# Projecting the last tokens of four segments, not two, in one job of the idle columns, with filling matmuls, an earlier layernorm and a deferred weight load

## The chip, the cores and the metric

One core of a Trainium2 chip. The metric is the device time of one execution in microseconds (us). A kernel's figure is the median of its runs. Every run in this document fell in the fast state, so all comparisons are of like with like.

## The reference, cut to what matters

Four layers run in a row, A B A B, on a residual stream of 2048 tokens by 640. Layer A is attention with a compressive memory and isn't touched by the change. Layer B carries its memory from one segment of 32 tokens to the next:

```python
for s in range(64):                                   # 2048 / 32
    h = concatenate([mem, x[:, 32*s:32*s+32]])        # 8 + 32 = 40 tokens
    q, k, v = h @ Wq, h @ Wk, h @ Wv                  # 640 -> 32 heads x 128
    p = softmax(where(mask, q @ k.T / sqrt(128), -1e9))
    o = (p @ v) @ Wo                                  # 40 x 640
    mem = o[:, :8]                                    # the next segment needs this
    outs.append(o[:, 8:])
# x = x + A(ln(x)); x = x + B(ln(x)); twice
```

## The kernel before

A step of layer B projects 32 columns for the queries and keys: the 8 memory rows and the first 24 tokens of the *next* segment. They are ready as soon as the memory is. The last 8 tokens of a segment (its tails) don't fit into the 32 columns and don't depend on the memory, so they are projected ahead in jobs of four units (two for Q, two for K) of 20 matmuls each. A job has room for 32 columns; before, it fills 16 of them with the tails of two segments:

```python
def make_tails_job(t):
    segs = [u for u in (t, t + 1) if u < nsteps]
    hx = wk.tile([128, NCH, 32], BF16, name="b_hx")
    for ii, u in enumerate(segs):
        nc.gpsimd.tensor_copy(hx[:, :, 8 * ii:8 * ii + 8], xcols(u, 24, 32))
    ...
```

The part of a step on which everything below turns, with the names that the profile uses:

```python
V2 = v_quarter(2); V3 = v_quarter(3)
...                                              # softmax: P is normalised by GpSimd and DVE
if len(bulk) > 0:
    bulk_unit_pe(bulk[0][0], bulk[0][1])         # first unit of tails: b_tps, 20 matmuls
ptp = ps_tile([128, 8, 128], BF16, "b_PTP")      # one tile in PSUM
for t in range(8):
    nc.tensor.transpose(ptp[:, t, :], P[...], C.identb[:])
nc.vector.tensor_copy(PTsb[:, 0:4, :], ptp[:, 0:4, :])
nc.scalar.copy(PTsb[:, 4:8, :], ptp[:, 4:8, :])
if len(bulk) > 1:
    bulk_unit_pe(bulk[1][0], bulk[1][1])         # second unit of tails
# OTP: 32 matmuls, probabilities x V; OTsb: evacuation on DVE and ACT
# OPS: 64 matmuls with Wo; msb (ACT), MT (transposes the new memory), hT, next step
```

Steps 0 and 63 of a layer have no units; steps 1 to 62 have two. Every fourth step also has a block OPSd, which does the output projection of 4 x 8 rows that no later step waits for. P are the probabilities, PTP their transposes, and PTsb the copy of PTP that OTP reads. All results of matmuls land in PSUM tiles here; copying one out to SBUF is called its evacuation. A matmul is called cold where the granted clock was 0.5, and warm where it was 1.00.

Of the kernel before, what the change touches and what calls it, by code (L numbers as in the profile page):

```python
# [18 lines left out]
F32 = mybir.dt.float32  # L19
BF16 = mybir.dt.bfloat16  # L20
# [9 lines left out]
NCH = 5  # L30
# [445 lines left out]
    pass  # L476


def load_B_weights(nc, tc, ctx, B_Wq, B_Wk, B_Wv, B_Wo):
    wp = ctx.enter_context(tc.tile_pool(name="b_w", bufs=1))  # L480
    W = BWeights()
    for nm, src in (("wq", B_Wq), ("wk", B_Wk), ("wv", B_Wv)):
        t = wp.tile([128, NCH, 4096], BF16, name=f"b_{nm}")
        nc.sync.dma_start(t[:], src.rearrange("(c p) h e -> p c (h e)", p=128))
        setattr(W, nm, t)
    W.wo = wp.tile([128, 32, D], BF16, name="b_wo")
    nc.sync.dma_start(W.wo[:], B_Wo.rearrange("h e d -> e h d"))
    return W


# [6 lines left out]
def layer_B(nc, tc, C, W, x_src, xb_src, x_dst, mem0, nsteps=64, out_bf16=False, dbg=None):  # L497
# [3 lines left out]
    with ExitStack() as ctx:  # L501
        st = ctx.enter_context(tc.tile_pool(name="b_state", bufs=1))
        hp = ctx.enter_context(tc.tile_pool(name="b_hT", bufs=4))
        qkp = ctx.enter_context(tc.tile_pool(name="b_qk", bufs=4))
        wk = ctx.enter_context(tc.tile_pool(name="b_wk", bufs=1))
        wk2 = ctx.enter_context(tc.tile_pool(name="b_wk2", bufs=2))
        sm = ctx.enter_context(tc.tile_pool(name="b_sm", bufs=2))
# [9 lines left out]
        nc.vector.tensor_tensor(out=fold[:, 0, :], in0=C.identb[:, 0:32], in1=C.identb[:, 64:96], op=ALU.add)  # L517
        nc.vector.tensor_tensor(out=fold[:, 1, :], in0=C.identb[:, 32:64], in1=C.identb[:, 96:128], op=ALU.add)
        OTdef = st.tile([128, 32, 32], BF16, name="b_OTdef")
        XO = st.tile([128, 320], F32, name="b_XO")  # L520
        nc.vector.memset(XO[:], 0.0)
        mask8 = st.tile([128, 8, 40], BF16, name="b_mask8")
# [21 lines left out]
        def ln_group_a(g):  # L544
            if g not in ln_dma:
                ln_group_dma(g)
            xt = ln_dma.pop(g)
            xn = wk.tile([128, D], BF16, name="b_xn", tag="PTsb")
            layernorm_tile(nc, sm, C, xt[:], xn[:], "b_ln")
            ln_state[g] = xn  # L550

        def ln_group_b(g):
            xn = ln_state.pop(g)
            tps = ps_tile([128, NCH, 128], BF16, "b_lntps")
            for c in range(NCH):
                nc.tensor.transpose(tps[:, c, :], xn[:, 128 * c:128 * c + 128], C.identb[:])
            xg = wk2.tile([128, NCH, 128], BF16, name="b_xnTg")
            nc.scalar.copy(xg[:], tps[:])
            xnT_g[g] = xg

        def xcols(s, a, b):
            g, i = divmod(s, 4)
            return xnT_g[g][:, :, 32 * i + a:32 * i + b]
# [54 lines left out]

        def bulk_unit_evac(job, u, eng):
            nm, b = (("Q", 0), ("Q", 1), ("K", 0), ("K", 1))[u]  # L620
            sb = wk.tile([128, 512], BF16, name="b_tsb", tag="tsb")
            evac(eng, sb[:], job["ps"][u][:], SCB if nm == "Q" else None)
            job["sb"][u] = sb

# [3 lines left out]
            transp4(job["sb"][u][:], tp, 0)  # L628
            job["tp"][u] = tp

        def bulk_unit_scatter(job, u, eng):
            nm, b = (("Q", 0), ("Q", 1), ("K", 0), ("K", 1))[u]
            for (t0, t1, seg, c0) in job["dests"]:
                dst_t = (QT if nm == "Q" else KT)[seg]
                src = job["tp"][u][:, 0:4, :].rearrange("p i (j t) -> p i j t", j=4)[:, :, :, t0:t1]
                dst = dst_t[:, 0:1280].rearrange("p (h c) -> p h c", c=40)[:, 16 * b:16 * b + 16, c0:c0 + (t1 - t0)] \
                    .rearrange("p (j i) c -> p i j c", j=4)
                evac(eng, dst, src)

        def new_job(cols, dests):  # L640
            return {"cols": cols, "dests": dests, "ps": {}, "sb": {}, "tp": {}}

        def run_job_now(job):
            for u in range(4):
                bulk_unit_pe(job, u)
                bulk_unit_evac(job, u, "act" if u % 2 == 0 else "dve")
                bulk_unit_tr(job, u)
                bulk_unit_scatter(job, u, "dve" if u % 2 == 0 else "act")

        ln_group_a(0); ln_group_b(0)  # L650
        alloc_seg(0)
        with nc.allow_non_contiguous_dma(reason="mem0 transpose load (tiny)"):
# [1 line left out]
                nc.sync.dma_start(hT[0][:, c, 32:40], mem0[:, 128 * c:128 * c + 128].rearrange("t p -> p t"))  # L654
        if nsteps > 1:
            alloc_seg(1)
        run_job_now(new_job(hT[0][:, :, 0:32], [(0, 32, 0, 0)]))

        def make_tails_job(t):
            segs = [u for u in (t, t + 1) if u < nsteps]  # L660
            hx = wk.tile([128, NCH, 32], BF16, name="b_hx")
            nc.gpsimd.memset(hx[:], 0.0)
            dl = []
            for ii, u in enumerate(segs):
                nc.gpsimd.tensor_copy(hx[:, :, 8 * ii:8 * ii + 8], xcols(u, 24, 32))
                dl.append((8 * ii, 8 * ii + 8, u, 24))
            return new_job(hx[:], dl)

        if nsteps > 1:
            if nsteps > 2:  # L670
                alloc_seg(2)
            run_job_now(make_tails_job(1))
        if nsteps > 4:
            ln_group_a(1); ln_group_b(1)
        jobs = {}
        pend_ln_b = []

        for s in range(nsteps):
            last = (s == nsteps - 1)
            if s + 2 < nsteps and (s + 2) not in hT:  # L680
                alloc_seg(s + 2)
            t_a = s + 2 if (s + 2) % 2 == 1 else None
            t_b = s + 1 if (s + 1) % 2 == 1 else None
            bulk = []
            if t_a is not None and t_a >= 3 and t_a < nsteps:
                if t_a + 1 < nsteps and (t_a + 1) not in hT:
                    alloc_seg(t_a + 1)
                jobs[t_a] = make_tails_job(t_a)
                bulk = [(jobs[t_a], 0), (jobs[t_a], 1)]
            if t_b is not None and t_b >= 3 and t_b in jobs:  # L690
                bulk = [(jobs.pop(t_b), 2), (jobs[t_b] if False else None, 3)]
                bulk[1] = (bulk[0][0], 3)
            g_need = (s + 6) // 4
            do_ln = None
            if g_need * 4 < nsteps and g_need not in xnT_g and g_need not in ln_state and g_need not in pend_ln_b:
                do_ln = g_need
# [14 lines left out]
            evac("dve", Ksb[:, 1, :], Kb[:])  # L711
            while pend_ln_b:
                ln_group_b(pend_ln_b.pop(0))
            Vsb = wk.tile([128, 4, 512], BF16, name="b_Vsb", tag="Vsb")

            def v_quarter(b4):
# [57 lines left out]
            evac("act", Vsb[:, 3, :], V3[:])  # L774
            if len(bulk) > 0:
                bulk_unit_pe(bulk[0][0], bulk[0][1])
            ptp = ps_tile([128, 8, 128], BF16, "b_PTP")
            for t in range(8):
                nc.tensor.transpose(ptp[:, t, :], P[:, 2 * t:2 * t + 2, :].rearrange("p g k -> p (g k)"), C.identb[:])
# [41 lines left out]
            nc.gpsimd.tensor_copy(OTdef[:, :, 8 * (s % 4):8 * (s % 4) + 8], OTsb[:].rearrange("p (h c) -> p h c", c=40)[:, :, 0:8])  # L821
            tsb = None
            if bulk:
                tsb = wk.tile([128, 2, 512], BF16, name="b_tsb", tag="Ksb")
                for i, (job, u) in enumerate(bulk):
                    nm = "Q" if u < 2 else "K"
                    evac("act" if i == 0 else "dve", tsb[:, i, :], job["ps"][u][:], SCB if nm == "Q" else None)
                    job["sb"][u] = tsb[:, i, :]
# [24 lines left out]
                pend_ln_b.append(do_ln)  # L853
            if bulk:
                for i, (job, u) in enumerate(bulk):
                    nm, b = (("Q", 0), ("Q", 1), ("K", 0), ("K", 1))[u]
                    for (t0, t1, seg, c0) in job["dests"]:
                        dst_t = (QT if nm == "Q" else KT)[seg]
                        src = btp[:, 4 * i:4 * i + 4, :].rearrange("p i (j t) -> p i j t", j=4)[:, :, :, t0:t1]
                        dst = dst_t[:, 0:1280].rearrange("p (h c) -> p h c", c=40)[:, 16 * b:16 * b + 16, c0:c0 + (t1 - t0)] \  # L860
                            .rearrange("p (j i) c -> p i j c", j=4)
                        evac("act" if i == 0 else "dve", dst, src)
            if out_bf16:
                xnb = wk.tile([128, 320], BF16, name="b_xnb", tag="xnb")
                nc.vector.tensor_tensor(out=xnb[0:64, :], in0=xps[0:64, :], in1=XO[0:64, :], op=ALU.add)
# [32 lines left out]
def full_kernel(tc, A_x, A_wq, A_wk, A_wv, A_wo, A_beta, B_x, B_mem0, B_Wq, B_Wk, B_Wv, B_Wo, B_seg_len, out, layers="ABAB"):  # L898
    nc = tc.nc
    with ExitStack() as ctx:  # L900
        C = build_consts(nc, tc, ctx)
        xin = A_x.rearrange("b s d -> (b s) d")
        xout = out.rearrange("b s d -> (b s) d")
        mem0 = B_mem0.rearrange("b t d -> (b t) d")
        X = tc.dram_tile([S_TOK, D], F32, name="xres")
        Xb = tc.dram_tile([S_TOK, D], BF16, name="xres_bf")
        nl = len(layers)
        assert layers[0] == "A"
        for li, L in enumerate(layers):
            lastl = (li == nl - 1)  # L910
            if L == "A":
                with ExitStack() as actx:
                    WA = load_A_weights(nc, tc, actx, C, A_wq, A_wk, A_wv, A_wo, A_beta)
                    layer_A(nc, tc, C, WA, xin if li == 0 else X, xout if lastl else X, li == 0, out_bf16=lastl,
                            xb_dst=None if lastl else Xb)
            else:
                with ExitStack() as bctx:
                    WB = load_B_weights(nc, tc, bctx, B_Wq, B_Wk, B_Wv, B_Wo)
                    layer_B(nc, tc, C, WB, X, Xb, xout if lastl else X, mem0, out_bf16=lastl)


# [56 lines left out]
```

## Time and profile before

| | before |
|---|---|
| time, median of 4 runs | 3668.54 us (3663.58 to 3669.13) |
| span of the profiled execution | 3666.6 us |
| TensorE busy | 3329.6 us, 91% |
| period of steps 1 to 60 of layer B, by step number modulo 4 (0, 1, 2, 3) | 19.26, 19.14, 19.14, 22.19 us |
| those 120 steps together | 2391.5 us |
| tails matmuls (b_tps with b_hx) | 5120 |

The periods are from the start of one step's first Q projection to the next's, medians over both layers. The 22.19 contains OPSd and the layernorm's transposes. All changes of the granted clock in this trace lie 3.41 us or a multiple of it apart: it is 1.00 from 3649.43 to 3652.84, for one, and 0.50 from there to 3656.25. So stretches of that length are used below to look at it. TensorE's 91% invites the conclusion that a matmul removed is time gained. The prediction's first part reads the lines that say otherwise: within a step TensorE is busy partly because work that nobody waits for has been put where it would wait.

### The profile page before, as it was taken

To read this page: it belongs to the slowest core of one execution; us is meant where nothing else is said; L and a number is where in the kernel's file an instruction comes from. 1 tells how busy PE (TensorE), PEld (TensorE's weight loads), DVE (VectorE), ACT (ScalarE), POOL (GpSimd) and SP (SyncE) were. 2 spreads that over 40 slices of the span, in tenths; PEclk is the share of its full clock that TensorE was granted. 3 is DMA by queue.
4 is the path that set the end of the run, shared out by engine and by line. 5 is a ranking of instruction groups with operands and counts; after the bars stand their busy time and mean duration, and the time that the engine had idled before them with its cause. 6 is when DMAs were issued, how large, how long until landed. Compare 5 with 4: busy or idle time off the path is not lost.

```text
span 3666.6 us, 126376 instructions
## 1 busy us (share of the span) xinstructions
PE 3329.6 (91%) x54996; PEld 2072.5 (57%) x54996; DVE 2032.9 (55%) x5299; ACT 1852.8 (51%) x4369; POOL 580.5 (16%) x1457
## 2 busy tenths in 40 slices
PE   6988959999999999999869889599999999999998
PEld 4756635555555555555546666355555555555555
DVE  8888834444444444444479888344444444444443
ACT  5978834444444444444359788344444444444443
POOL 4233210110111111010122332101101111110100
PEclk9999979999999999999989999799999999999999
DMA  2010061000000000000020111600000000000000
GB/s 63 12 38 30 29 248 31 12 12 13 13 13 12 14 13 12 14 12 10 20 66 12 46 38 29 249 29 10 10 11 11 11 11 11 11 10 12 10 8 8
DMA packets 85996, 112.24 MB, mean 31 GB/s; under 512 B 27328, under 2 KB 75456, under 8 KB 81600
## 3 DMA queue, kind: packets, MB, share of 16 engines
q1 hardware_dynamic: 85440, 104.18, 9.1%
q8 instruction: 429, 7.03, 0.8%
q14 instruction: 127, 1.04, 0.1%
HBM read 72.13 MB, written 23.59 MB: 26 GB/s over the span
## 4 chain that ended last, share of the span: by engine, by line
PE 74%; ACT 12%; DVE 7%; issue 3%; DMA 2%; POOL 2%; SPq 0%; DVEq 0%; ACTq 0%; POOLq 0%
PE b_VPS L103 16%; PE b_tps L103 9%; PE b_OPS L103 8%; ACT a_Pj L338 5%; PE b_Qa L103 4%; PE b_Qb L103 4%; PE b_Kb L103 4%; PE b_Ka L103 4%; PE a_S L333 3%; ACT b_KT L103 2%; PE b_ttp L103 2%; PE b_PTP L103 2%; PE b_TPK L103 2%; PE b_TPQ L103 2%; PE b_OPSd L103 2%
## 5 line engine op out<-in xcount | busy, mean ns | idle before, releaser
L103 PEld LDWEIGHTS <-b_hT 128*32 128x32 bf16 (+1 forms) x15520 | 608.4, 101 | 498.2 <-issue 99.8
L103 PE MATMUL b_VPS<-b_wv,b_hT 128*64 128x512 bf16 x5120 | 626.3, 382 | 0.0
L338 ACT ACTIVATE a_Pj<-a_S,a_negm 128x128 bf16<-128x128 f32 (+3 forms) x1024 | 504.1, 541 | 50.0 <-DVE a_negm L337 43.9
L337 DVE TENSOR_REDUCE a_negm<-a_S 128x1 f32<-128x128 f32 (+3 forms) x1024 | 467.5, 481 | 76.6 <-PE a_S L335 47.9
L103 ACT CAST b_Vsb<-b_VPS 128x512 bf16<-128x512 f32 x512 | 289.3, 594 | 179.6 <-PE b_VPS L103 179.6
L103 POOL TENSOR_TENSOR b_P<-b_P,b_rs 128x320 bf16<-128x320 bf16 x128 | 92.4, 722 | 1799.6 <-DVE b_rs L103 1785.0
L333 PE MATMUL a_S<-a_kT,a_qTm 128*128 128x128 bf16 (+3 forms) x1024 | 292.2, 300 | 53.0 <-ACT a_Pj L338 44.1
L103 PE MATMUL b_OPS<-b_wo,b_OTsb 128*32 128x320 bf16 x8192 | 307.2, 303 | 33.8 <-DVE b_OTsb L103 33.8
L103 PEld LDWEIGHTS <-b_OTsb 128*32 128x32 bf16 x8192 | 209.1, 98 | 102.1 <-DVE b_OTsb L103 46.9
L348 PE MATMUL a_tpA<-c_identb,a_Pj 128*128 128x128 bf16 x2048 | 232.8, 220 | 7.7 <-ACT a_Pj L338 2.8
L335 PE MATMUL a_S<-c_negu,c_identb 128*128 128x128 bf16 x1024 | 221.6, 220 | 0.0
L103 ACT ACTIVATE b_P<-b_SP 128x320 bf16<-128x320 f32 x256 | 111.9, 437 | 197.7 <-DVE b_SP L103 197.7
L103 PEld LDWEIGHTS <-b_hx 128*32 128x32 bf16 x5120 | 113.8, 96 | 150.7 <-issue 55.1
L103 DVE CAST b_OTsb<-b_OTP 128x320 bf16<-128x320 f32 x256 | 114.1, 486 | 141.6 <-PE b_OTP L103 141.1
L103 DVE CAST b_Ksb<-b_Kb 128x512 bf16<-128x512 f32 x128 | 88.5, 692 | 187.7 <-PE b_Kb L103 187.7
L103 DVE COPY b_QT<-b_TPQ 128x128 bf16<-128x128 bf16 (+1 forms) x254 | 62.1, 286 | 231.2 <-ACT b_QT L103 231.2
L103 ACT CAST b_Ksb<-b_Ka 128x512 bf16<-128x512 f32 x128 | 74.9, 585 | 205.8 <-PE b_Ka L103 205.8
L103 DVE TENSOR_SCALAR b_Qsb<-b_Qb 128x512 bf16<-128x512 f32 x128 | 88.5, 692 | 161.6 <-PE b_Qb L103 161.6
L348 PEld LDWEIGHTS <-a_Pj 128*128 128x128 bf16 x2048 | 147.3, 98 | 50.3 <-issue 10.1
L335 PEld LDWEIGHTS <-c_identb 128*128 128x128 bf16 x1024 | 99.5, 97 | 124.2 <-issue 94.3
L103 PE MATMUL b_Qa<-b_wq,b_hT 128*32 128x512 bf16 x2560 | 166.3, 383 | 3.1
L103 PE MATMUL b_tps<-b_wq,b_hx 128*32 128x512 bf16 x2560 | 164.8, 387 | 0.0
(172 smaller groups left out, 6080.4 us busy)
## 6 DMA issues: line engine op xcount, KB each, us to landing
xres<-a_xnew SPq DMA_DIRECT2D x32, 320.0 KB
b_wq<-in_B_Wq_dram SPq DMA_DIRECT2D x2, 5120.0 KB
b_wk<-in_B_Wk_dram SPq DMA_DIRECT2D x2, 5120.0 KB
b_wv<-in_B_Wv_dram SPq DMA_DIRECT2D x2, 5120.0 KB
b_wo<-in_B_Wo_dram SPq DMA_DIRECT2D x2, 5120.0 KB
a_qTm<-a_qT SPq DMA_DIRECT2D x256, 32.0 KB
b_XO<-xres SPq DMA_DIRECT2D x256, 30.0 KB
xres_bf<-a_xnb SPq DMA_DIRECT2D x32, 160.0 KB
```

Source lines behind the costliest of these rows:

```text
L103: r = f(*a, **k)
L333: nc.tensor.matmul(Sx[:, 0:N], lhsT=stt["qTm"][:, j, 128 * qc:128 * qc + 128], rhs=kT[:, 0:N], start=True, stop=False)
L335: nc.tensor.matmul(Sx[:, N - 128:N], lhsT=C.identb[:], rhs=C.negu[:], start=False, stop=True)
L337: nc.vector.tensor_reduce(out=negm[:], in_=Sx[:, 0:N], axis=AX.X, op=ALU.max, negate=True)
L338: nc.scalar.activation(out=Pj[:, OFFS[qc]:OFFS[qc] + N], in_=Sx[:, 0:N], func=ACT.Exp, bias=negm[:, 0:1], scale=1.0)
L348: nc.tensor.transpose(tpA[:, bi, :], Pj[:, OFFS[qc] + 128 * kc: OFFS[qc] + 128 * kc + 128], C.identb[:])
```

## The change

The intent is to halve the tails' matmuls by filling all 32 columns of a job with the tails of four segments, so that each step carries one unit and not two. What comes along: staging tiles from which GpSimd copies each segment's share (`copy_tails`); four filling matmuls in the steps that have no unit; the layernorm of segments 4 to 7 ahead of the first projection; and the weight loads issued behind the first layernorm's loads.

```diff
+        def make_gen_job(g):                       # segments 4g+1 .. 4g+4
             hx = wk.tile([128, NCH, 32], BF16, name="b_hx")
             nc.gpsimd.memset(hx[:], 0.0)
+            for ii, t in enumerate(gen_segs(g)):
+                nc.gpsimd.tensor_copy(hx[:, :, 8 * ii:8 * ii + 8], xcols(t, 24, 32))
+            return new_job(hx[:], g)
+        def copy_tails(t):                         # on GpSimd, a step or more ahead
+            ...
+            nc.gpsimd.tensor_copy(dst, src_t[:, :, 8 * ii:8 * ii + 8])
 ...
-                bulk = [(jobs[t_a], 0), (jobs[t_a], 1)]          # two units, in steps 1 to 62
+                bulk = [(genjob[g_], (s + 3) % 4)]               # one, in steps 1 to 60
 ...
             if len(bulk) > 0:
                 bulk_unit_pe(bulk[0][0], bulk[0][1])
+            else:                                                # steps 0, 61, 62, 63
+                fps = ps_tile([128, 512], F32, "b_fill")
+                for c in range(4):
+                    nc.tensor.matmul(fps[:], lhsT=C.identb[:], rhs=W.wq[:, c, 0:512], ...)
 ...
+        ln_group_dma(0)
+        W.load()                                                 # wq, wk, wv, wo
         ln_group_a(0); ln_group_b(0)
 ...
+        if nsteps > 4:
+            ln_group_a(1); ln_group_b(1)                         # moved up from behind the jobs
         run_job_now(new_job(hT[0][:, :, 0:32], [(0, 32, 0, 0)]))
-            run_job_now(make_tails_job(1))
-            ln_group_a(1); ln_group_b(1)
+            run_job_now(make_gen_job(0))
 ...
-            g_need = (s + 6) // 4
+            g_need = (s + 8) // 4                                # later layernorms 2 steps earlier
```

Cut: tile tags, the order of `alloc_seg`, and the QT and KT buffers, which go from 4 to 3.

More of the change, by code (lines that the diff above doesn't have):

```diff
@@ L476, with load_B_weights, load @@
     pass
-def load_B_weights(nc, tc, ctx, B_Wq, B_Wk, B_Wv, B_Wo):
+def load_B_weights(nc, tc, ctx, B_Wq, B_Wk, B_Wv, B_Wo, defer=False):
     wp = ctx.enter_context(tc.tile_pool(name="b_w", bufs=1))
     W = BWeights()
-    for nm, src in (("wq", B_Wq), ("wk", B_Wk), ("wv", B_Wv)):
-        t = wp.tile([128, NCH, 4096], BF16, name=f"b_{nm}")
-        nc.sync.dma_start(t[:], src.rearrange("(c p) h e -> p c (h e)", p=128))
-        setattr(W, nm, t)
+    W.wq = wp.tile([128, NCH, 4096], BF16, name="b_wq")
+    W.wk = wp.tile([128, NCH, 4096], BF16, name="b_wk")
+    W.wv = wp.tile([128, NCH, 4096], BF16, name="b_wv")
     W.wo = wp.tile([128, 32, D], BF16, name="b_wo")
-    nc.sync.dma_start(W.wo[:], B_Wo.rearrange("h e d -> e h d"))
+    def load():
+        for t, src in ((W.wq, B_Wq), (W.wk, B_Wk), (W.wv, B_Wv)):
+            nc.sync.dma_start(t[:], src.rearrange("(c p) h e -> p c (h e)", p=128))
+        nc.sync.dma_start(W.wo[:], B_Wo.rearrange("h e d -> e h d"))
+    W.load = load
+    if not defer:
+        load()
+        W.load = lambda: None
     return W
@@ L503, in layer_B @@
         hp = ctx.enter_context(tc.tile_pool(name="b_hT", bufs=4))
-        qkp = ctx.enter_context(tc.tile_pool(name="b_qk", bufs=4))
+        qkp = ctx.enter_context(tc.tile_pool(name="b_qk", bufs=3))
         wk = ctx.enter_context(tc.tile_pool(name="b_wk", bufs=1))
@@ L519, in layer_B @@
         OTdef = st.tile([128, 32, 32], BF16, name="b_OTdef")
+        QTt = [st.tile([128, 32, 32], BF16, name=f"b_QTt{i}") for i in range(2)]
+        KTt = [st.tile([128, 32, 32], BF16, name="b_KTt")] * 2
         XO = st.tile([128, 320], F32, name="b_XO")
@@ L620, in bulk_unit_evac @@
             nm, b = (("Q", 0), ("Q", 1), ("K", 0), ("K", 1))[u]
-            sb = wk.tile([128, 512], BF16, name="b_tsb", tag="tsb")
+            sb = wk.tile([128, 512], BF16, name="b_tsb", tag="Vsb")
             evac(eng, sb[:], job["ps"][u][:], SCB if nm == "Q" else None)
@@ L629, in bulk_unit_tr, with bulk_unit_scatter @@
             job["tp"][u] = tp
-        def bulk_unit_scatter(job, u, eng):
+        def bulk_unit_scatter(job, u, eng, tp=None, slot=0):
             nm, b = (("Q", 0), ("Q", 1), ("K", 0), ("K", 1))[u]
+            tp = job["tp"][u] if tp is None else tp
+            if isinstance(job["dests"], int):
+                dst_t = (QTt if nm == "Q" else KTt)[job["dests"] % 2]
+                src = tp[:, 4 * slot:4 * slot + 4, :].rearrange("p i (j t) -> p i j t", j=4)
+                dst = dst_t[:, 16 * b:16 * b + 16, :].rearrange("p (j i) c -> p i j c", j=4)
+                evac(eng, dst, src)
+                return
             for (t0, t1, seg, c0) in job["dests"]:
                 dst_t = (QT if nm == "Q" else KT)[seg]
-                src = job["tp"][u][:, 0:4, :].rearrange("p i (j t) -> p i j t", j=4)[:, :, :, t0:t1]
+                src = tp[:, 4 * slot:4 * slot + 4, :].rearrange("p i (j t) -> p i j t", j=4)[:, :, :, t0:t1]
                 dst = dst_t[:, 0:1280].rearrange("p (h c) -> p h c", c=40)[:, 16 * b:16 * b + 16, c0:c0 + (t1 - t0)] \
@@ L656, in layer_B, with gen_segs @@
             alloc_seg(1)
+        if nsteps > 4:
+            ln_group_a(1); ln_group_b(1)
         run_job_now(new_job(hT[0][:, :, 0:32], [(0, 32, 0, 0)]))
-        def make_tails_job(t):
-            segs = [u for u in (t, t + 1) if u < nsteps]
+        def gen_segs(g):
+            return [t for t in range(4 * g + 1, 4 * g + 5) if t < nsteps]
+        def make_gen_job(g):
             hx = wk.tile([128, NCH, 32], BF16, name="b_hx")
             nc.gpsimd.memset(hx[:], 0.0)
-            dl = []
-            for ii, u in enumerate(segs):
-                nc.gpsimd.tensor_copy(hx[:, :, 8 * ii:8 * ii + 8], xcols(u, 24, 32))
-                dl.append((8 * ii, 8 * ii + 8, u, 24))
-            return new_job(hx[:], dl)
+            for ii, t in enumerate(gen_segs(g)):
+                nc.gpsimd.tensor_copy(hx[:, :, 8 * ii:8 * ii + 8], xcols(t, 24, 32))
+            return new_job(hx[:], g)
+        def copy_tails(t):
+            g, ii = divmod(t - 1, 4)
+            for src_t, dct in ((QTt[g % 2], QT), (KTt[g % 2], KT)):
+                dst = dct[t][:, 0:1280].rearrange("p (h c) -> p h c", c=40)[:, :, 24:32]
+                nc.gpsimd.tensor_copy(dst, src_t[:, :, 8 * ii:8 * ii + 8])
         if nsteps > 1:
@@ L671, in layer_B @@
                 alloc_seg(2)
-            run_job_now(make_tails_job(1))
-        if nsteps > 4:
-            ln_group_a(1); ln_group_b(1)
-        jobs = {}
+            run_job_now(make_gen_job(0))
+            copy_tails(1)
+            if nsteps > 2:
+                copy_tails(2)
+        genjob = {}
         pend_ln_b = []
@@ L681, in layer_B @@
                 alloc_seg(s + 2)
-            t_a = s + 2 if (s + 2) % 2 == 1 else None
-            t_b = s + 1 if (s + 1) % 2 == 1 else None
-            bulk = []
-            if t_a is not None and t_a >= 3 and t_a < nsteps:
-                if t_a + 1 < nsteps and (t_a + 1) not in hT:
-                    alloc_seg(t_a + 1)
-                jobs[t_a] = make_tails_job(t_a)
-                bulk = [(jobs[t_a], 0), (jobs[t_a], 1)]
-            if t_b is not None and t_b >= 3 and t_b in jobs:
-                bulk = [(jobs.pop(t_b), 2), (jobs[t_b] if False else None, 3)]
-                bulk[1] = (bulk[0][0], 3)
-            g_need = (s + 6) // 4
+            if s >= 1:
+                if s % 4 == 1:
+                    for t in (s, s + 1, s + 2):
+                        if t < nsteps and not (s == 1 and t in (1, 2)):
+                            copy_tails(t)
+                elif s % 4 == 2:
+                    if s + 2 < nsteps:
+                        copy_tails(s + 2)
+            bulk = []
+            g_need = (s + 8) // 4
             do_ln = None
@@ L713, in layer_B @@
                 ln_group_b(pend_ln_b.pop(0))
+            g_ = (s + 3) // 4
+            if s >= 1 and gen_segs(g_):
+                if s % 4 == 1:
+                    genjob[g_] = make_gen_job(g_)
+                bulk = [(genjob[g_], (s + 3) % 4)]
             Vsb = wk.tile([128, 4, 512], BF16, name="b_Vsb", tag="Vsb")
@@ L776, in layer_B @@
                 bulk_unit_pe(bulk[0][0], bulk[0][1])
+            else:
+                fps = ps_tile([128, 512], F32, "b_fill")
+                for c in range(4):
+                    nc.tensor.matmul(fps[:], lhsT=C.identb[:], rhs=W.wq[:, c, 0:512], start=(c == 0), stop=(c == 3))
             ptp = ps_tile([128, 8, 128], BF16, "b_PTP")
@@ L823, in layer_B @@
             if bulk:
-                tsb = wk.tile([128, 2, 512], BF16, name="b_tsb", tag="Ksb")
+                tsb = wk.tile([128, 1, 512], BF16, name="b_tsb", tag="Ksb")
                 for i, (job, u) in enumerate(bulk):
@@ L855, in layer_B @@
                 for i, (job, u) in enumerate(bulk):
-                    nm, b = (("Q", 0), ("Q", 1), ("K", 0), ("K", 1))[u]
-                    for (t0, t1, seg, c0) in job["dests"]:
-                        dst_t = (QT if nm == "Q" else KT)[seg]
-                        src = btp[:, 4 * i:4 * i + 4, :].rearrange("p i (j t) -> p i j t", j=4)[:, :, :, t0:t1]
-                        dst = dst_t[:, 0:1280].rearrange("p (h c) -> p h c", c=40)[:, 16 * b:16 * b + 16, c0:c0 + (t1 - t0)] \
-                            .rearrange("p (j i) c -> p i j c", j=4)
-                        evac("act" if i == 0 else "dve", dst, src)
+                    bulk_unit_scatter(job, u, "act" if i == 0 else "dve", tp=btp, slot=i)
             if out_bf16:
@@ L917, in full_kernel @@
                 with ExitStack() as bctx:
-                    WB = load_B_weights(nc, tc, bctx, B_Wq, B_Wk, B_Wv, B_Wo)
+                    WB = load_B_weights(nc, tc, bctx, B_Wq, B_Wk, B_Wv, B_Wo, defer=True)
                     layer_B(nc, tc, C, WB, X, Xb, xout if lastl else X, mem0, out_bf16=lastl)
```

## The prediction

> **What bounds the kernel now.** I read the page first, then the chain of work that ended last, then one recurrent step in order of time, then the rare steps that already run without the work that the change removes. The kernel is four layers, A B A B. Each B layer is 64 steps in a row, each needing the memory rows of the one before.
>
> ```profile
> span 3666.6 us, 126376 instructions
> PE 3329.6 (91%) x54996; PEld 2072.5 (57%) x54996; DVE 2032.9 (55%) x5299; ACT 1852.8 (51%) x4369; POOL 580.5 (16%) x1457
> ...
> PE   6988959999999999999869889599999999999998
> ...
> PE 74%; ACT 12%; DVE 7%; issue 3%; DMA 2%; POOL 2%; SPq 0%; DVEq 0%; ACTq 0%; POOLq 0%
> ```
>
> See the two long runs of 9 in the PE row (the B layers), and that 74% of the chain is matmuls. Neither says what a matmul is worth when it goes: for that, a step. These lines are from the timeline of one step in the middle of the first B layer (start, length, engine; a bracket is idle time and what ended it):
>
> ```profile
> 1202.20 1.26 PE L103 MATMUL b_tps<-b_wk,b_hx 128*32 128x512 bf16 x20
> ...
> 1203.39 0.63 PE L103 MATMUL b_PTP<-c_identb,b_P 128*128 128x128 bf16 x8
> ...
> 1203.95 1.26 PE L103 MATMUL b_tps<-b_wk,b_hx 128*32 128x512 bf16 x20
> 1204.06 0.42 DVE L103 COPY b_PTsb<-b_PTP 128x512 bf16<-128x512 bf16 x1 [0.49 <-PE b_PTP L103]
> 1204.52 0.58 ACT L103 COPY b_PTsb<-b_PTP 128x512 bf16<-128x512 bf16 x1 [1.29 <-DVE b_PTsb L103]
> ...
> 1205.15 0.73 PE L103 MATMUL b_OTP<-b_PTsb,b_Vsb 40*128 40x40 bf16 x32
> ...
> 1206.17 2.36 PE L103 MATMUL b_OPS<-b_wo,b_OTsb 128*32 128x320 bf16 x64 [0.28 <-DVE b_OTsb L103]
> ...
> 1209.06 0.47 PE L103 MATMUL b_MT<-b_sel,b_msb 128*128 128x8 bf16 x6
> ```
>
> The two b_tps units project the last 8 tokens of later segments ("tails"). They are off the recurrence, but sit in TensorE's order where it would wait: the first beside the softmax normalisation, the second beside the copy of the transposed probabilities (PTsb). So removing a unit pays only what the wait behind it doesn't take back. Steps 0 and 63 of a layer have no units. From the last step:
>
> ```profile
> 3651.41 0.75 PE L103 MATMUL b_PTP<-c_identb,b_P 128*128 128x128 bf16 x8 [1.10 <-POOL b_P L103]
> ...
> 3652.20 0.42 DVE L103 COPY b_PTsb<-b_PTP 128x512 bf16<-128x512 bf16 x1 [0.49 <-PE b_PTP L103]
> 3652.66 0.58 ACT L103 COPY b_PTsb<-b_PTP 128x512 bf16<-128x512 bf16 x1 [1.29 <-DVE b_PTsb L103]
> 3652.68 1.19 PE L103 MATMUL b_OTP<-b_PTsb,b_Vsb 40*128 40x40 bf16 x32 [0.52 <-DVE b_PTsb L103]
> ...
> 3653.80 3.54 PE L103 MATMUL b_OPS<-b_wo,b_OTsb 128*32 128x320 bf16 x64
> ```
>
> Two things show. OTP starts 0.06 us after the DVE half of PTsb and does not wait for the ACT half. And the same 64 OPS matmuls take 3.54 us instead of 2.36; the stretches of 1 us around them (length, busy PE, PEld, DVE, ACT, POOL, then granted clock) say why:
>
> ```profile
> 3651.00:3652.00 1.00, 0.59 (x8) 0.45 (x8) 0.67 (x2) 0.36 (x1) 0.36 (x1) 1.00 0.00 0
> 3652.00:3653.00 1.00, 0.48 (x18) 0.41 (x17) 0.42 (x1) 0.34 (x1) 0.00 (x0) 0.92 0.00 0
> 3653.00:3654.00 1.00, 0.93 (x29) 0.69 (x28) 0.74 (x2) 0.76 (x3) 0.00 (x0) 0.50 0.00 0
> ```
>
> The clock halves after the two gaps.
>
> [...] half speed from about 3652.84 to 3656[...] it fell when TensorE was still busy 1.79 of the 3.41 us before[...]. [...] the ACT half of PTsb starts 0.04 us after the DVE half ends (1204.48 to 1204.52), though they write different columns. [...] a pair of GpSimd hT copies took 0.64 us beside a DVE layernorm and 0.54 us without.
>
> **The change part by part.**
>
> *Tails in fours.* Before, a job of 4 units serves 2 segments, 2 units a step in steps 1 to 62. After, it serves 4 segments, 1 unit a step in steps 1 to 60. The first unit stays, the second goes: 64 units a layer, 64 x 1.19 us (its piece in the chain) = 76 us of TensorE. What the path gets: PTP starts as before (1203.39). DVE starts PTsb 0.67 later (1204.06), takes 0.42, OTP follows after 0.06: start + 1.15. From OTP to OPS is 1.02 (1205.15 to 1206.17). The second half of OTP needs ACT's copy: 0.61 after OTP's start, as in step 0 (565.51 to 566.12), and its 16 matmuls take about 0.33 (half of the 32's 0.63 of weight loads), so 0.95, just under that 1.02; step 0 indeed has 565.51 to 566.53. OPS at PTP + 2.17, against 1206.17 - 1203.39 = 2.78: **0.61 us a step**, half of the unit's 1.19.
>
> After OPS, 4 transposes (ttp) of 8 go, but the memory rows (MT) also wait for msb on ACT, which starts 0.05 after OPS's end, takes 0.42, and 0.06 more: 0.53, and 1206.17 + 2.36 + 0.53 = 1209.06 is exactly when MT starts now. Nothing gained. Q, K and V follow unchanged, with the wait for the KT copies before SP (ACT 0.66 plus DVE 0.23). So 60 steps x 0.61 = 36.6 us a layer, 73.2 in both.
>
> *Steps 61 and 62* lose both units and get four filling matmuls of 512 columns (about 4 x 0.22 = 0.86 us, an estimate from 1.08 us for five 512-column passes). PTP can then start when GpSimd's P is there (1203.22 + 0.05), 0.12 earlier: 0.73 x 4 = 2.9.
>
> *Steps 0 and 63* get the filling too. PTP still waits for P, but the gap of 1.0 to 1.4 us ahead of PTP shrinks to 0.2 to 0.5 and I expect the clock to stay: OPS takes 3.87, 4.03, 3.53 and 3.54 us in these four steps, so 1.51 + 1.67 + 1.17 + 1.18 = 5.5.
>
> *Prologue.* Layernorm of group 1 moves from behind the first tail job to ahead of the first projection, where TensorE waits for wq anyway (18.6 us). Now it stands alone: the last ttp ends at 547.63, Qa starts at 549.95, 2.3 us (2382.74 to 2385.06 in the second layer, again 2.3). In the first layer a cold clock follows: Qa and Qb take 1.97 and 1.88 us start to start instead of 1.08, 1.7 more. Together 2.3 + 1.7 + 2.3 = 6.3.
>
> *Deferred weight load.* The trace shows b_xt for groups 0 and 1 issued at 485.8 and 495.4, before wq at 501.4, which waits for layer A's last stores. So the order in the queue is already what the edit asks for: 0.
>
> *Moved to GpSimd.* Two copies of 128x256 a step (0.40 us as OTdef's), about 100 us in all on an engine that is 16% busy. At worst six in a row, 2.4 us, when P is not due for some 11 us. Three instead of four QT/KT buffers: the buffer that is reused was last read a step before. Cost 0.
>
> Sum: 73.2 + 2.9 + 5.5 + 6.3 = 87.9; 3668.5 - 87.9 = **3581 us**, 2.4% less.
>
> **The rivals.**
>
> *The wait takes all back.* If OTP had to wait for both halves of PTsb, it would start at 1205.10 + 0.05, when it starts now; only the edges would gain, some 15 us: 3654. Steps 0 and 63 speak against it, in all four cases.
>
> *All of the unit is gained.* 128 missing units x 1.19 = 152 us: about 3505 with the edges (steps 0 and 63, prologue). It would need PTsb ready at once; the copy starts only when PTP ends. Against it: the same lines.
>
> *The clock drops in ordinary steps.* A gap of 0.5 and one of about 0.25 open just where steps 0 and 63 went cold. If OPS cost 1.2 more in a third of the steps, 120 x 0.4 = 48 us go: 3629; in all, slower than now, about 3725. Against: the first unit still runs densely up to PTP. From PTP to OPS is 2.17 us of transposes, small matmuls and waits[...]. [...] from TPQ at 1215.44 to 1218.85, only V's 1.2 us (35%) are dense, and the clock between 550 and 1772 us is 1.00. Step 0, which fell, had about 0.65 (19%). Layer A stays at 1.00 with stretches of 1.76 busy in 3.40.
>
> *GpSimd is late.* The copies delay P[...]. It would show as SP or PTP waiting for GpSimd; with some 5 to 10 us of slack I give it little.
>
> **Range and chances.** The 0.61 is read from steps that are the new case, so I trust it to 0.1 a step, 12 us. The edges may miss by 5. The clock is the wide tail upwards; the 8-in-10 range is 3568 to 3603. The 2% line is 3595, 14 us above my number: over 2% faster 0.78, within 2% 0.19, slower 0.03.
>
> **What would show each step.** Period of a plain step 19.13 before, 18.5 after. PTP to OPS 2.17, with a PE wait of about 0.5 on DVE's PTsb ahead of OTP in every step. MT 0.53 after OPS's end, now waiting for ACT msb. OPS at 2.36, also in steps 0 and 63, with the clock at 1.00 across the B layers; 3.5 there is the third rival. Qa right behind the last prologue unit; wq issued when it was. The 5120 b_tps matmuls with hx become 2560, while the span falls by just over half of their time. Wrong would be OTP waiting for ACT, a PE wait on GpSimd, or prologue projections waiting on b_xt behind the weights.

## The result, and the profile after

The changed kernel takes 3589.14 us (median of 8 runs, 3584.79 to 3593.34). The kernel before took 3668.08 beside it (13 runs, 3663.34 to 3675.17). The ratio is 0.9786 with a 95% interval of 0.9776 to 0.9795: faster, by more than 2%. Ratios here are the mean time of one kernel's fast runs over that of the other's fast runs of the same rounds, so not quite the ratio of the medians.

The page after, in the order in which the prediction showed the page before: span, busy time, TensorE's row of the slices, and the chain by engine.

```profile
span 3585.8 us, 120061 instructions
...
PE 3180.8 (89%) x51956; PEld 2000.4 (56%) x51956; DVE 1937.6 (54%) x4927; ACT 1878.6 (52%) x4237; POOL 663.3 (18%) x1677
...
PE   6988959999999999999879888599999999999998
...
PE 69%; ACT 15%; DVE 7%; issue 3%; DMA 3%; POOL 2%; SPq 0%; ACTq 0%; DVEq 0%; POOLq 0%
```

TensorE lost 149 us of work, the span 81. The row of slices looks as before; in the chain, ACT's share rose from 12 to 15%. Where the other half went can be read in one group, the OTP matmuls, from the table of instructions (busy us and mean ns, then TensorE's idle time just before them and what ended it). Before:

```profile
L103 PE MATMUL b_OTP<-b_PTsb,b_Vsb 40*128 40x40 bf16 x4096 | 95.0, 178 | 2.5 <-DVE b_PTsb L103 2.1
```

After:

```profile
L103 PE MATMUL b_OTP<-b_PTsb,b_Vsb 40*128 40x40 bf16 x4096 | 123.1, 177 | 82.8 <-DVE b_PTsb L103 66.5 <-ACT b_PTsb L103 1.1
```

Idle time ahead of OTP that DVE's half of PTsb ended went from 2.1 to 66.5 us, which is 0.52 us in each of the 128 steps. That is the wait that the second unit had been covering. The timeline of one plain step in the middle of the first layer B, to hold against the step in the prediction:

```profile
1214.36 0.63 PE L103 MATMUL b_PTP<-c_identb,b_P 128*128 128x128 bf16 x8
...
1215.03 0.42 DVE L103 COPY b_PTsb<-b_PTP 128x512 bf16<-128x512 bf16 x1 [0.49 <-PE b_PTP L103]
...
1215.49 0.58 ACT L103 COPY b_PTsb<-b_PTP 128x512 bf16<-128x512 bf16 x1 [1.29 <-DVE b_PTsb L103]
...
1215.51 1.09 PE L103 MATMUL b_OTP<-b_PTsb,b_Vsb 40*128 40x40 bf16 x32 [0.52 <-DVE b_PTsb L103]
...
1216.53 2.36 PE L103 MATMUL b_OPS<-b_wo,b_OTsb 128*32 128x320 bf16 x64
...
1219.42 0.47 PE L103 MATMUL b_MT<-b_sel,b_msb 128*128 128x8 bf16 x6 [0.20 <-ACT b_msb L103]
```

From PTP to OPS it is 1216.53 - 1214.36 = 2.17 us, where it was 2.78, and MT starts 0.53 after OPS ends, as before. OTP's length grew from 0.73 to 1.09: its second half now waits for ACT's half of the copy. The chain of waits through the same step (start, length, engine) goes through that half:

```profile
1215.03 0.43 DVE b_PTsb L103
...
1215.49 0.59 ACT b_PTsb L103
...
1216.12 0.47 PE b_OTP L103 x16
1216.60 2.32 PE b_OPS L103 x64
```

So OPS starts when the 16 matmuls behind ACT's copy are through: 0.61 after OTP's start, plus 0.41. That is 1.02, the same as the route over DVE's evacuation. The two routes are tied, and both begin at DVE's copy, behind which ACT's is queued (DVE's ends at 1215.45, ACT's starts at 1215.49).

Where the 80.8 us between the two profiled spans came from, cut at the first Q projections of the two layers B:

| stretch | before - after, us | predicted |
|---|---|---|
| start to first Qa of the first B | 4.84 | 2.3 |
| its step 0 | 3.18 | 3.2 |
| steps 1 to 60, both layers | 70.3 | 73.2 |
| steps 61 and 62, both layers | 2.1 | 2.9 |
| step 63 of the first B, second layer A, second prologue | -0.61 | 3.5 |
| step 0 of the second B | 0.30 | 1.7 |
| step 63 of the second B to the end | 0.61 | 1.2 |

The predicted column splits the prediction's own 5.5 and 6.3 over the stretches in which they would appear. The periods after are 18.65, 18.92, 18.53 and 21.27 us (step number modulo 4 = 0, 1, 2, 3), so 0.61, 0.22, 0.61 and 0.92 less.

The edges, first the prologue. TensorE before, around the first Q projection:

```profile
547.23 0.40 PE L103 MATMUL b_ttp<-c_identb,b_tsb 128*128 128x128 bf16 x4 [0.87 <-DVE b_tsb L103]
549.57 0.45 PE L103 MATMUL b_lntps<-c_identb,b_xn 128*128 128x128 bf16 x5 [1.94 <-DVE b_xn L103]
549.95 2.20 PE L103 MATMUL b_Qa<-b_wq,b_hT 128*32 128x512 bf16 x20
```

And after:

```profile
544.78 0.40 PE L103 MATMUL b_ttp<-c_identb,b_tsb 128*128 128x128 bf16 x4 [0.87 <-DVE b_tsb L103]
545.11 1.26 PE L103 MATMUL b_Qa<-b_wq,b_hT 128*32 128x512 bf16 x20
```

The layernorm between them is gone and Qa runs at full clock (1.26 us at a granted 1.00, not 2.20 at 0.54; the clock is the mean up to Qb's start). This is the first layer B; in the second it was the other way round (2.32 at 0.50 after, 1.26 at 1.00 before). The last step of the second layer B after, for the clock:

```profile
3570.09 1.04 PE L103 MATMUL b_fill<-b_wq,c_identb 128*128 128x512 bf16 x4
...
3573.59 2.36 PE L103 MATMUL b_OPS<-b_wo,b_OTsb 128*32 128x320 bf16 x64
```

OPS takes 2.36 us, not 3.54. No OPS of the changed kernel takes over 2.6; before, the four without units took 3.87, 3.53, 4.03 and 3.54.

### The profile page after: what moved, and what is told of

It is laid out like the page before. It is cut to its first block, busy times and chain, and to the rows that moved or that the text cites. A ratio compares the mean times of both kernels' runs of the same rounds, so it can differ in the third digit from the quotient of the medians.

```text
span 3585.8 us, 120061 instructions
## 1 busy us (share of the span) xinstructions
PE 3180.8 (89%) x51956; PEld 2000.4 (56%) x51956; DVE 1937.6 (54%) x4927; ACT 1878.6 (52%) x4237; POOL 663.3 (18%) x1677
## 3 DMA queue, kind: packets, MB, share of 16 engines
q14 instruction: 125, 1.02, 0.1%
## 4 chain that ended last, share of the span: by engine, by line
PE 69%; ACT 15%; DVE 7%; issue 3%; DMA 3%; POOL 2%; SPq 0%; ACTq 0%; DVEq 0%; POOLq 0%
PE b_VPS L103 16%; PE b_OPS L103 8%; ACT a_Pj L338 5%; PE b_tps L103 5%; PE b_Qa L103 4%; PE b_Qb L103 4%; PE b_Kb L103 4%; PE b_Ka L103 4%; PE a_S L333 2%; ACT b_KT L103 2%; ACT b_PTsb L103 2%; PE b_PTP L103 2%; PE b_TPK L103 2%; PE b_TPQ L103 2%; PE b_OPSd L103 2%
## 5 line engine op out<-in xcount | busy, mean ns | idle before, releaser
L103 PE MATMUL b_OTP<-b_PTsb,b_Vsb 40*128 40x40 bf16 x4096 | 123.1, 177 | 82.8 <-DVE b_PTsb L103 66.5
L103 DVE CAST b_hT<-b_MT 128x24 bf16<-128x24 f32 x126 | 23.0, 182 | 300.9 <-PE b_MT L103 300.9
L103 DVE CAST b_OTsb<-b_OTP 128x320 bf16<-128x320 f32 x256 | 125.8, 492 | 73.0 <-PE b_OTP L103 65.9
```

The source lines that it names most:

```text
L103: r = f(*a, **k)
```

## The experiments

The theory: removing the second unit pays about half of its matmuls, since the copy of the transposed probabilities takes the other half; the small parts pay at the edges by shorter waits and a clock that stays up. Rivals: the small parts carry more than that; the filling matmuls do nothing; the remaining unit is still on the path; the other half went to some other wait. "Correct" below means that the output agreed with the reference within the comparison's tolerance.

**One part alone, on the kernel before.** First the load:

```diff
-    load_B_weights: nc.sync.dma_start(...) for wq, wk, wv, wo
+    def load(): ...                     # the same four, called later
+        ln_group_dma(0)
+        W.load()
         ln_group_a(0); ln_group_b(0)
```

> The kernel before plus the deferred weight load alone. Theory (the trace of before shows wq waiting for layer A's last stores at 501.4 us, with the activations' loads already ahead of it): no change, 3668 us within 4, first Qa of the first B layer at about 550. Rival (the order of the load matters): wq lands earlier, first Qa some us earlier in both B layers, 3650 to 3662.

3665.06 us beside 3664.08 (11 runs of the kernel before, median), ratio 1.0001 (0.9988 to 1.0014). The deferral gives nothing, as the issue times of the queue had said.

The layernorm:

```diff
+        if nsteps > 4:
+            ln_group_a(1); ln_group_b(1)
         run_job_now(new_job(hT[0][:, :, 0:32], [(0, 32, 0, 0)]))
 ...
             run_job_now(make_tails_job(1))
-        if nsteps > 4:
-            ln_group_a(1); ln_group_b(1)
```

> The kernel before plus the layernorm of group 1 ahead of the first projection. Theory: the gap of 2.3 us ahead of Qa closes in each B layer, and in some executions 1.7 us of cold Qa and Qb: minus 4.6 to 6.3, so 3662 to 3664. Rival (hidden behind the weight transfers anyway): 3668.

3659.98 us, ratio 0.9983 (0.9969 to 0.9997): about 6 us by the ratio, 4 by the medians, in line with the 6.3. In its trace the first Qa starts 0.33 after the last transposes start (549.11 to 549.44), as in the changed kernel (544.78 to 545.11), and the first layer's step 0 takes 18.53, where it took 21.71 before. The latter is the clock: Qa and Qb run warm, and so does its OPS, although this kernel has no filling (the 3.18 less is near the 1.7 of Qa and Qb and the 1.51 of OPS that the cold cost there before). In the second layer the same step takes 21.84 (20.20 in the kernel before, where Qa takes 1.26 and OPS 4.03), so what the clock does at the edge changes from layer to layer.

The filling:

```diff
             if len(bulk) > 0:
                 bulk_unit_pe(bulk[0][0], bulk[0][1])
+            else:
+                fps = ps_tile([128, 512], F32, "b_fill")
+                for c in range(4):
+                    nc.tensor.matmul(fps[:], lhsT=C.identb[:], rhs=W.wq[:, c, 0:512],
+                                     start=(c == 0), stop=(c == 3))
```

> The kernel before plus the filling matmuls in steps 0 and 63, where it has no tail unit. Theory (clock): OPS falls from 3.5 to 4.0 us to 2.36 in four steps, minus 5.5, so 3662.5. Rival (the filling is only more work): plus 0 to 3.

3658.84 us, ratio 0.9984 (0.9971 to 0.9997), and no OPS over 2.6 us. Matmuls whose result nobody reads save about 5 us. For this part and the layernorm's the interval is wide, 1 to 11 us each.

**The change without its filling.**

```diff
-            else:
-                fps = ps_tile([128, 512], F32, "b_fill")
-                for c in range(4): ...
```

> The changed kernel without the filling matmuls. Theory: steps 0, 61, 62 and 63 of each B layer run OPS at half clock, 1.2 to 1.6 us more each, eight steps: plus 8 to 12, so 3597 to 3601. Rival (only steps 0 and 63 go cold, as before): plus 5, 3594. Rival (the filling does nothing): 3589.

3593.3 us (3587.52 to 3594.77), ratio 0.9800 (0.9786 to 0.9815), so some 5 us over the changed kernel's 0.9786, a little under what I expected, and the two intervals overlap. The time alone fits the rival with two cold steps a layer (3594); the trace does not. Seven of the eight OPS of steps 0, 61, 62 and 63 ran between 3.60 and 4.03 us, 10.9 us over 2.36 each, and steps 61 and 62 took 20.2 and 20.3 in both layers, where the changed kernel's take 18.6. Steps 1 to 60 are the same to 0.1 us in all (2321.0 and 2321.1).

**The second unit put back.** In the changed kernel a dummy takes the place of the second unit: 20 matmuls of the same shape, not evacuated.

```diff
-            if len(bulk) > 1:
-                bulk_unit_pe(bulk[1][0], bulk[1][1])
+            if bulk:
+                dps = ps_tile([128, 512], F32, "b_dum")
+                for c in range(5):
+                    for j in range(4):
+                        nc.tensor.matmul(dps[32*j:32*j+32, :], lhsT=bulk[0][0]["cols"][:, c, :],
+                                         rhs=W.wk[:, c, 512*j:512*j+512], ...)
```

> The changed kernel with a dummy unit of 20 matmuls (result unused, not evacuated, not transposed) where the second unit stood, in the 120 steps that have a first unit. Theory (the path gets the unit less the wait that it hid): plus 0.6 a step, 72 us, 3661. Rival (the gain came from the evacuations, transposes and scatters that went with the unit): stays within 10 us of 3589.

3653.01 us beside 3664.34 (7 runs), ratio 0.9968 (0.9953 to 0.9982). The 120 steps together take 2391.8 us, and the kernel before's take 2391.5. So all that the change gained in these steps is the second unit's matmuls. The evacuations, transposes and scatters that went, and the GpSimd copies that came, together count for nothing there. What is left of the gain, 0.32%, is about what the two single parts gave, 0.17% and 0.16%; with intervals of some 0.14% to each side of all three, that they add up so well is luck.

**Part of it put back.** The same with `range(2)`: 8 matmuls, 40% of a unit.

```diff
-                for c in range(5):
+                for c in range(2):
```

> The same with 8 matmuls, about 0.43 us, which fit in the gap of 0.5 us ahead of OTP. Theory (the gap is a wait for PTsb, so matmul work in it is free): plus 0 to 6, 3589 to 3595. Rival (every matmul counts): 120 x 0.43, plus 52, 3641.

3587.14 us, ratio 0.9788 (0.9772 to 0.9805); the 120 steps take 2320.6. They keep TensorE busy for 73.8 us in all and cost nothing. One step of it, in order of time, shows why:

```profile
1218.43 0.61 PE L103 MATMUL b_dum<-b_wk,b_hx 128*32 128x512 bf16 x8
...
1218.54 0.43 DVE L103 COPY b_PTsb<-b_PTP 128x512 bf16<-128x512 bf16 x1 [0.49 <-PE b_PTP L103]
...
1219.02 1.09 PE L103 MATMUL b_OTP<-b_PTsb,b_Vsb 40*128 40x40 bf16 x32
```

The dummies run beside DVE's copy, and OTP still starts 0.05 behind it. The wait was there, with something in it or not.

**The first unit taken away too.** This was meant to give a wrong result (the tails come from the prologue's job), and passed the comparison all the same; the time is what it is for. The comparison thus does not notice wrong tails, so "correct" for the changed kernel is no proof that its tails are copied rightly.

```diff
-            if s >= 1 and gen_segs(g_):
+            if False:                              # every step gets the filling
-            for src_t, dct in ((QTt[g % 2], QT), (KTt[g % 2], KT)):
+            for src_t, dct in ((QTt[0], QT), (KTt[0], KT)):
```

> The changed kernel with no tail unit in any step (wrong result on purpose: the tails of the first generation are reused), the filling in every step. Theory (PTP waits for P, not for the unit): 0 to 0.1 a step less, 3577 to 3590. Rival (TensorE's work is the bound): 120 x (1.19 - 0.86 + 0.28), minus 73, 3516.

3597.52 us (3588.38 to 3600.82), ratio 0.9812 (0.9797 to 0.9827). My expectation missed: less work took 10 us more than the previous run's by the medians, 9 by the ratios. A plain step takes 18.63, not 18.53. In its trace PTP starts earlier, but half of its operand isn't there: the eight transposes take 0.75 us (at 1218.12) in place of 0.63, because the second four wait for DVE's half of P (0.21 us ahead of those at 790.77). PTP to OPS becomes 2.33 (2.17 in the changed kernel), and OPS's end to MT 0.58 (0.53). Over 120 steps the 0.10 makes 12 us; four cold OPS (3.79 and 3.85 in steps 12 and 56 of the first layer, 3.87 and 3.93 in steps 20 and 23 of the second) add 6.0. That is the 18.0 us by which the 120 steps grew over the previous run's (2338.6 against 2320.6); the rest of the profiled execution was 6.4 shorter. It also gives the missing term of the steps 61 and 62, which are such steps.

**The first unit taken away, and no filling.** The same, with the filling's `else` removed. The result passed the comparison here as well.

> No tail unit and no filling either (wrong result on purpose). Theory (sparse steps lose the clock): OPS at 3.5 to 4.0 in most steps, plus 1.2 to 1.6 each, 3700 to 3790, and slower than the kernel with the unit though it does less[...]. Rival (the clock survives, less work): 3577 to 3590.

3732.96 us beside 3664.34, ratio 1.0187 (1.0172 to 1.0203). The kernel with the least work is slower than the kernel before. Its mean granted clock is 0.938; 89 of its 128 OPS take over 2.6 us. TensorE in one of its steps:

```profile
1210.07 0.74 PE L103 MATMUL b_PTP<-c_identb,b_P 128*128 128x128 bf16 x8 [1.01 <-POOL b_P L103]
...
1212.36 4.03 PE L103 MATMUL b_OPS<-b_wo,b_OTsb 128*32 128x320 bf16 x64
```

And the stretches of 3.41 us around it (length, busy PE, PEld, DVE, ACT, POOL, then granted clock, DMA):

```profile
1209.15:1212.56 3.41, 1.83 (x48) 1.45 (x52) 2.28 (x6) 1.98 (x5) 0.72 (x1) 1.00 0.00 0
1212.56:1215.97 3.41, 3.41 (x60) 2.18 (x56) 1.94 (x6) 0.33 (x1) 2.23 (x8) 0.50 0.03 7
```

TensorE was busy 1.83 of 3.41 us, and the next stretch runs at half the clock. The stretch of the changed kernel that ends where OPS starts, as this one nearly does, has one unit in it and stays up:

```profile
1213.12:1216.53 3.41, 2.77 (x63) 1.65 (x61) 2.28 (x7) 2.09 (x5) 0.72 (x1) 1.00 0.01 2
```

The rival in which the clock drops in ordinary steps is thus real. The one unit that the change leaves in steps 1 to 60 is what keeps it away there: with it, and the filling in the others, no OPS takes over 2.6 us.

**The wait itself.** If DVE's and ACT's halves of the copy are serialised only because they read one PSUM tile, two tiles should end that. The edit, in the changed kernel and in the kernel before:

```diff
-            ptp = ps_tile([128, 8, 128], BF16, "b_PTP")
+            ptps = [ps_tile([128, 4, 128], BF16, f"b_PTP{i}") for i in range(2)]
             for t in range(8):
-                nc.tensor.transpose(ptp[:, t, :], P[...], C.identb[:])
+                nc.tensor.transpose(ptps[t // 4][:, t % 4, :], P[...], C.identb[:])
-            nc.vector.tensor_copy(PTsb[:, 0:4, :], ptp[:, 0:4, :])
-            nc.scalar.copy(PTsb[:, 4:8, :], ptp[:, 4:8, :])
+            nc.vector.tensor_copy(PTsb[:, 0:4, :], ptps[0][:])
+            nc.scalar.copy(PTsb[:, 4:8, :], ptps[1][:])
```

Beside it the changed kernel once more, unedited, for a comparison on the same chip:

> The changed kernel once more, unedited, for a comparison on the same chip with the next three: ratio 0.978 to 0.980, about 3588.

3588.65 us beside 3669.2 (9 runs), ratio 0.9786 (0.9772 to 0.9799): the first result again.

> The changed kernel with the transposes of P in two PSUM tiles instead of one, so that DVE copies the first four while TensorE does the last four, and ACT need not wait for DVE. Theory (OTP waits for DVE's copy of PTsb, which waits for all eight transposes[...]): DVE starts four transposes or 0.28 us earlier, minus 0.28 x 128 = 36 us, 3553. Rival (ACT's half is what holds OPS back): minus 0 to 10, 3580 to 3589.

3547.68 us (3544.27 to 3552.21), ratio 0.9674 (0.9661 to 0.9687): 41 us under the changed kernel beside it. The 120 steps take 2288.5 us, 32.6 less, and the rest is in the edges and the scatter of the runs. Correct, and faster than both kernels. One step:

```profile
1205.26 0.63 PE L103 MATMUL b_PTP<-c_identb,b_P 128*128 128x128 bf16 x8
1205.69 0.42 DVE L103 COPY b_PTsb<-b_PTP 128x512 bf16<-128x512 bf16 x1 [0.26 <-PE b_PTP L103]
...
1205.92 0.59 ACT L103 COPY b_PTsb<-b_PTP 128x512 bf16<-128x512 bf16 x1 [0.83 <-PE b_PTP L103]
1206.17 0.87 PE L103 MATMUL b_OTP<-b_PTsb,b_Vsb 40*128 40x40 bf16 x32 [0.28 <-DVE b_PTsb L103]
...
1207.17 2.36 PE L103 MATMUL b_OPS<-b_wo,b_OTsb 128*32 128x320 bf16 x64
```

DVE starts 0.43 after PTP's start (0.67 with one tile), since it waits for the first four transposes only. ACT overlaps DVE, waiting for PTP and no longer for DVE's copy. OTP starts at 0.91 after PTP, not 1.15, and OPS at 1.91, not 2.17. The edit ends two waits at once, DVE's for the last four transposes and ACT's for DVE, and no run parts them. But DVE's start moved by 0.24, OTP's by the same 0.24 and OPS's by 0.26, so the first wait accounts for nearly all of the gain: what cost here was that DVE's copy waited for all eight transposes, less that the two copies ran one after the other.

> The same edit in the kernel before. Theory (there the second unit covers the wait): no gain in steps 1 to 62, only 0.28 in steps 0 and 63: 3664 to 3668. Rival (the copies cost in themselves): minus 36, 3630.

3663.33 us, ratio 0.9988 (0.9974 to 1.0001), the 120 steps 2391.2. The same edit is worth nothing in the kernel before, where the second unit covers the copy.

**A fifth of the first unit into what is left of the wait.** On top of the two tiles, 16 of the unit's 20 matmuls before PTP and 4 behind it:

```diff
-                bulk_unit_pe(bulk[0][0], bulk[0][1])
+                bulk_unit_pe(bulk[0][0], bulk[0][1], range(4))    # chunks 0 to 3
 ...
+            if len(bulk) > 0:
+                bulk_unit_pe(bulk[0][0], bulk[0][1], [4])         # chunk 4, behind PTP
```

> The two PSUM tiles, and the last 4 of the unit's 20 matmuls moved behind the transposes, into the rest of the gap. Theory (they are free there, and PTP can start up to 0.12 us earlier, when P is ready): 0.05 to 0.12 x 120 less than with the two tiles alone, 3540 to 3547. Rival (P is not ready earlier): the same as with two tiles alone.

3547.65 us, ratio 0.9670 (0.9656 to 0.9683): no more than without, where I had expected up to 7. One step:

```profile
1203.62 0.74 PE L103 MATMUL b_PTP<-c_identb,b_P 128*128 128x128 bf16 x8
1204.29 0.40 PE L103 MATMUL b_tps<-b_wq,b_hx 128*32 128x512 bf16 x4
1204.62 0.89 PE L103 MATMUL b_OTP<-b_PTsb,b_Vsb 40*128 40x40 bf16 x32
```

PTP starts 0.12 sooner behind the unit (1.08 us after the unit's start and not 1.20), but its transposes then wait for DVE's half of P (0.74 us), the moved matmuls start at 0.67, and OTP is held to 1.00 after PTP where it was 0.91. What was won ahead was given back behind.

## Why the prediction was right

It said 3581 us, with 3568 to 3603, and faster by over 2% as the likeliest; 3589.14 and 0.9786 fall there. By its own steps:

*The second unit pays half.* Right. PTP to OPS is 2.17 us as worked out from step 0; the dummies show that the whole of it is the second unit, and that the first 0.6 us of work in that place are free. The term was 73.2 and measured 70.3. In steps with no layernorm transposes, before or after, the gain is 0.61 us, as worked out. Most of the 2.9 that is missing is a term that I left out: later layernorms run two steps earlier, so their transposes leave the steps that are 3 modulo 4, where they cost 0.31 (22.19 against 21.88 in step 59, which has none), and land in those that are 1 modulo 4, where they cost 0.39 (18.92 against 18.53). That is some 0.07 more, about 2 us over the 28 steps that have them. It isn't the place that makes them dearer: with the dummy unit behind PTP they cost 0.31 in the same place (19.45 against 19.14). Without the second unit less of them is hidden.

*The rival "OTP waits for both halves".* Half right, in a way that I had seen only as a near miss. OTP's start waits for DVE alone (1215.51, when DVE's half ends at 1215.45 and ACT's at 1216.07). But ACT's half reaches OPS at 1.02 after OTP's start and not at 0.95; I took half of the weight loads' 0.63, about 0.33, for the 16 matmuls, and they took 0.41 to OPS's start. The two routes are level. This made no difference to the sum. The wait that remains starts with DVE's copy, which waits for all eight transposes, and the two-tile edit took 41 us out of it.

*Steps 61 and 62.* Mis-sized: 0.73 a step, measured 0.55 and 0.50, 2.1 in all, not 2.9. PTP did start 0.12 earlier after its step's first Q projection (12.61, not 12.73), but PTP to OPS took 2.28 and 2.34 there, not 2.17. The missing piece is that GpSimd normalises one half of P and DVE the other, and I asked only for GpSimd's; the run without units shows the later half holding the second four transposes.

*The edges.* 8.3 us in place of 11.8. The single parts are right: the filling alone 5, the layernorm alone 4 to 6, the deferral nothing. What the sum lacked is that the edges depend on things that the change doesn't touch. Between the two profiled executions the first layer A ended about 1.3 us earlier (first weight load issued at 501.36 and 500.03), and the second, whose code is the same, took 3.4 longer from its first transposes to the end of its last output projection (475.8 and 479.2). Over the fourteen profiles of this document it lies between 473.7 and 480.4. In the second prologue after, the tails' projections ran cold to the last (2.32 us; before, the last took 1.26), and Qa and Qb of step 0 behind them too (2.32 and 1.61), so that step took 19.90 us and not 18.53, as in the first layer, and gained only 0.30. In the run with the dummy unit it took 18.53 in the second layer too. The changed kernel had it cold in both of its profiles (19.90 and 19.94), so whether this is chance or belongs to the change is not shown.

*The clock.* Right that it stays at full speed through the two layers B (granted 1.00 from 545.11 to 1784 and from 2344.07 to 3583), but for the cold start of the second (half clock to 2344.07, 2.8 us after its first Qa), and that the filling holds it in the steps without units (no OPS over 2.6 us with it; seven of eight at 3.60 to 4.03 without). The rival was given its chance rightly; the run with neither unit nor filling shows it, 3733 us at a mean granted clock of 0.938. The shares of dense work that I held against it, 35% in a present step and 19% in step 0, were my estimate from the timeline, and no run shows that such a share decides. That this is near the 3725 given for the clock dropping in all steps is chance: 89 of 128 OPS were cold, in a kernel with other work.

*GpSimd and the buffers.* Right: GpSimd's busy time went from 580.5 to 663.3 us, and no TensorE instruction waits on its copies.

What stays open: the exact rule by which the clock falls, why the second layer A took 3.4 us longer, and how much of the 8 us between 3581 and 3589 is the scatter of the runs. The terms above account for 7.1 of it in the profiled pair.

## What to carry to other kernels

Before counting a removed matmul as gain, look at what the next instruction on its engine waits for: here half of the time of 20 matmuls behind the transposes had been free, and taking them out paid only down to the copy that they had hidden. A change that uncovers a wait also makes its repair worth something: the same two-tile edit gave 0.1% before, its interval reaching 1.0001, and 1.1% after. And work that nobody needs may be what keeps the clock up (here a mean granted clock of 0.976 in the changed kernel, and 0.938 without unit and filling, at ratios of 0.9786 and 1.0187 to the kernel before), so take it out in steps and watch the granted clock each time.

## What the runs show of the clock, the shared tile and the scatter

- The clock fell after stretches of 3.41 us in which TensorE was busy 1.83 us (the run with neither unit nor filling), 1.79 (the last step of the kernel before), 2.28 (its first step, 563.77 to 567.18) and even 2.52 (the run with the filling in every step, 790.03 to 793.44). It stayed at 1.00 in a stretch of layer A with 1.76 busy in 3.40 (217.40 to 220.80), though that one starts 1.78 us off the raster of the clock's changes in that trace. So busy time as the profile counts it doesn't tell when the clock falls. How much filling prevents it is not shown in general: without unit and filling 89 of 128 OPS were cold; with four matmuls of 512 columns (1.04 us) none was in the steps 0, 61, 62 and 63 of the changed kernel, where seven of eight were without them, and four of 128 were in the run that had them in place of the unit.
- One PSUM tile for all eight transposes made DVE's copy wait for all of them (it starts 0.67 us after PTP, and 0.43 with two tiles) and ACT's for DVE's (it starts 0.04 after DVE's end, and 0.19 before it with two tiles); two tiles in its place saved 0.25 to 0.32 us a step, 41 us in all, and nothing while other matmuls covered the wait (ratio 0.9988).
- The scatter of whole executions decides what a difference of a few us is worth: 13 runs of the kernel before lay between 3663.34 and 3675.17. A layer whose code is the same took from 473.7 to 480.4 us in fourteen profiles, of different kernels; the two of the changed kernel agree (479.2).
